# Choosing between VectorE and GpSimd: by estimate for every instruction, or fixed except near the barriers

## Chip, cores and metric

One core of one Trainium2 chip. The metric is device microseconds of that core for one execution of the whole kernel; lower is better. For a core that works alone there is no second die to compare with, so a run counts as fast when it is within 1.5% of the fastest of its kernel.

## The reference

Two layers; each adds a linear attention with softmax features and then a gated feed-forward network without an activation, both behind a layer normalisation. S = 2048 tokens, D = 576, H = 32 heads of Dh = 18, F = 4608, all in bf16. Both layers use the same weights.

```python
pq = q @ w_phi ; pk = k @ w_phi                           # per head, 18 x 18
phi_q = concat([softmax(pq), softmax(-pq)], axis=-1)      # the same for phi_k
kv  = phi_k^T @ v ; z = sum over tokens of phi_k          # needs all tokens
o   = (phi_q @ kv) / (phi_q @ z + 1e-6)
x   = x + o @ wo                                          # attention, of layernorm(x)
x   = x + ((x_ln @ w_gate) * (x_ln @ w_up)) @ w_down      # feed-forward, x_ln = layernorm(x)
# twice
```

Because `kv` sums over all tokens, every layer has a **K phase** (all tokens' features of K), a **barrier** (kv complete), and then **Q tiles** (128 tokens each, 16 of them), which feed **feed-forward blocks** (two tiles each, 8 per layer). Layer 2's K tiles are worked off as layer 1's blocks end; its barrier comes after layer 1's last block.

## The kernel before

The kernel is a program of tasks (Python generators) that a **list scheduler** places on the engines when the kernel is built. Each operation carries an estimated duration in ns; the scheduler takes the operation that could start earliest (tasks of priority 10 and 11 get a head start of 300 and 800 ns), a task's priority breaks ties and decides who gets a free buffer first, and the instruction streams are then fixed in that order.

A request `"alt"` names several engines; the one whose estimated finish is earliest gets the work (VectorE's estimate is weighted by 1.2):

```python
for eng, ops in r[1]:
    ...
    e_ = max(self.free_at[eng], tr.ready_time(deps), th.t_ready)
    f_ = e_ + sum(o.dur for o in ops) * self.alt_cost[eng]
    if pick is None or f_ < pick[0]:
        pick = (f_, e_, eng, ops)
```

Every K or Q tile passes through `softmax_front`. Each tile has two branches, softmax(p) and softmax(-p), of 128 x 576:

```python
def softmax_front(self, st_, pz, Wm, km):
    ...                                        # projection on TensorE, copy to psb on ScalarE, max and min on VectorE
    yield ("alt", [(eng, [Op(dur, ... tensor_tensor(d1, p3, mxb, ALU.subtract) ...)])      # L861, first difference
                   for eng, dur in (("pool", 1170), ("dve", 675))])
    for h in range(2):
        yield ("alt", [(eng, [Op(dur, ... tensor_tensor(d2h, ph, mnbh, ALU.subtract) ...)])  # L868, second, in halves
                       for eng, dur in (("pool", 620), ("dve", 375))])
    ...                                        # exp on ScalarE, sums on VectorE (L880), reciprocal on ScalarE
    for br in range(2):
        yield ("alt", [(eng, [Op(dur, ... tensor_tensor(ev, ev, rb, ALU.mult) ...)])         # L894, scaling
                       for eng, dur in (("pool", 1150), ("dve", 675))])
```

The layer normalisation `t_ln` ends with such a choice too (L804, estimates 800 on GpSimd and 280 on VectorE).

After its front, a Q tile transposes both branches on TensorE (L1020), ScalarE copies them (L1023), TensorE multiplies by kv (L1041), VectorE divides (L1066, one buffer `o`), TensorE transposes the result (L1077), ScalarE copies it to `oT` (L1082), and TensorE projects it (L837). The gate and up products of a block are L1130, the down projection L1197 and L1200.

Who starts Q tiles, and when:

```python
self.NPS, ... self.NO = 3, ..., 1              # 3 softmax buffers psb, 1 buffer o
self.pace = (8, 4)                             # layer 1, layer 2
def t_q(self, L):
    for b in range(NB):                        # NB = 8 pairs of tiles
        ...
        if b >= self.pace[L - 1]:              # pair b waits for the end of feed-forward block b - pace
            yield ("wait", ("x2", L, b - s.pace[L - 1]))
        if b >= s.early // 2:
            yield ("wait", ("BD", L))          # the barrier
        for j in range(2):
            yield ("go", s.t_aout(L, 2 * b + j), (4 if b == 0 else 7) + (NS - 2 * b - j) / 100.0, ...)
        ...                                    # cut: the pair's normalisation; from pair 1 on, a wait until the pair before is done
```

## Time and profile before

| | before |
|---|---|
| median of the first 3 runs | 1230.62 us (1229.88 to 1232.37) |
| end of layer 1's K phase (last L925 of it) | 104.9 us |
| first feed-forward matmul (first L1130) | 133.98 us |
| block starts, layer 1, blocks 2 to 7 | 61.3 to 62.0 us apart |
| block starts, layer 2, blocks 2 to 5 | 63.8 to 63.9 us apart |

The lines of the page, the stages and the groups stand in the prediction. Timeline columns: start, duration, engine, line, operation, how often; in brackets the idle time before it and what ended it. Every Q tile has one L1082 copy, when its output is ready for the last projection.

```profile
114.06 0.69 ACT L1082 COPY oT<-ps 128x640 bf16<-128x640 bf16 x1 [2.19 <-PE ps L1077]
126.46 0.69 ACT L1082 COPY oT<-ps 128x640 bf16<-128x640 bf16 x1 [0.90 <-PE ps L1077]
...
133.98 0.28 PE L1130 MATMUL ps<-xT,Wg 64*128 64x256 bf16 x1 [0.78 <-ACT xT L818]
```

Block 0 starts at 134.

The four scalings of one pair of layer 2's Q tiles, the timeline of the kernel before from 909 to 913 us, GpSimd and VectorE:

```profile
909.17 1.16 POOL L894 TENSOR_TENSOR dd<-dd,ss 128x576 bf16<-128x576 bf16 x1 [2.60 <-ACT ss L888]
909.85 2.74 DVE L894 TENSOR_TENSOR dd<-dd,ss 128x576 bf16<-128x576 bf16 x2
910.58 1.39 POOL L894 TENSOR_TENSOR dd<-dd,ss 128x576 bf16<-128x576 bf16 x1 [0.25 <-ACT ss L888]
```

VectorE's two take 2.74 us where two of 0.745 would take 1.5: both engines work by turns. TensorE's waits in layer 2's Q blocks, 732 to 1056 us, before (total, times, longest):

```profile
PE ps L1020 <- DVE dd L894: 4.5, 5, 1.1
PE ps L1197 <- DMA wdr<-in_B_w_down_dram: 4.3, 9, 1.0
PE ps L1020 <- POOL dd L894: 1.3, 2, 1.2
```

### The profile page before, as it was taken

To read this page: it belongs to the slowest core of one execution; us is meant where nothing else is said; L and a number is where in the kernel's file an instruction comes from. 1 tells how busy PE (TensorE), PEld (TensorE's weight loads), DVE (VectorE), ACT (ScalarE), POOL (GpSimd) and SP (SyncE) were. 2 spreads that over 40 slices of the span, in tenths; PEclk is the share of its full clock that TensorE was granted. 3 is DMA by queue.
4 is the path that set the end of the run, shared out by engine and by line. 5 is a ranking of instruction groups with operands and counts; after the bars stand their busy time and mean duration, and the time that the engine had idled before them with its cause. 6 is when DMAs were issued, how large, how long until landed. Compare 5 with 4: busy or idle time off the path is not lost.

```text
span 1227.8 us, 33685 instructions
## 1 busy us (share of the span) xinstructions
PE 1131.8 (92%) x15202; PEld 846.5 (69%) x15202; DVE 663.3 (54%) x1243; ACT 460.1 (37%) x1080; POOL 233.3 (19%) x225
## 2 busy tenths in 40 slices
PE   5775999998999999999999589999999999999998
PEld 3553786875858585858586368685867677767684
DVE  7898658679444444444446684836353635422131
ACT  6766446364323232323224444424242424212120
POOL 4686205234020202020203320302010101000000
PEclk8888899999999999999999789999999999999999
DMA  8372006216150515151514101604334342433414
GB/s 190 85 270 93 2 22 167 33 42 160 31 164 24 165 23 163 25 158 30 156 31 137 39 2 27 154 29 124 83 99 98 88 108 74 123 89 97 137 50 145
DMA packets 126249, 114.61 MB, mean 93 GB/s; under 512 B 44826, under 2 KB 124954, under 8 KB 124954
## 3 DMA queue, kind: packets, MB, share of 16 engines
q1 hardware_dynamic: 126106, 112.48, 33.7%
q8 instruction: 118, 1.93, 0.7%
q14 instruction: 25, 0.20, 0.1%
HBM read 100.59 MB, written 2.36 MB: 84 GB/s over the span
## 4 chain that ended last, share of the span: by engine, by line
PE 71%; DVE 14%; DMA 9%; ACT 3%; POOL 1%; issue 1%; SPq 0%; DVEq 0%; ACTq 0%
PE ps L1130 45%; PE ps L1197 10%; PE ps L837 9%; DMA wdr<-in_B_w_down_dram 9%; DVE dd L894 3%; DVE ss L880 2%; DVE dd L868 2%; DVE mxmn L856 2%; DVE mxmn L854 1%; PE ps L1200 1%; DVE st L782 1%; PE ps L1041 1%; PE ps L1020 1%; DVE xln L804 1%; PE ps L925 1%; PE ps L1077 1%
## 5 line engine op out<-in xcount | busy, mean ns | idle before, releaser
L1130 PE MATMUL ps<-xT,Wu 64*128 64x256 bf16 x4608 | 571.2, 270 | 2.0 <-DVE hT L1175 1.8
L1130 PE MATMUL ps<-xT,Wg 64*128 64x256 bf16 x4608 | 571.0, 270 | 1.6 <-ACT xT L818 1.6
L1130 PEld LDWEIGHTS ps<-xT,Wg 64*128 64x128 bf16 x4608 | 430.3, 94 | 33.8 <-issue 3.6
L1130 PEld LDWEIGHTS ps<-xT,Wu 64*128 64x128 bf16 x4608 | 432.5, 94 | 30.2 <-DVE hT L1175 3.1
L1175 DVE TENSOR_TENSOR hT<-ps,gsb 128x512 bf16<-128x512 f32 x288 | 198.6, 691 | 333.6 <-ACT gsb L1173 333.4
L1173 ACT CAST gsb<-ps 128x512 bf16<-128x512 f32 x288 | 168.5, 585 | 505.1 <-PE ps L1130 504.5
L1197 PE MATMUL ps<-wdr,hT 128*128 128x512 bf16 x1152 | 311.1, 381 | 15.9 <-DMA wdr<-in_B_w_down_dram 14.4
L1200 PE MATMUL ps<-wdr,hT 128*128 128x64 bf16 x1152 | 221.9, 193 | 0.0
L1197 PEld LDWEIGHTS ps<-wdr,hT 128*128 128x128 bf16 x1152 | 112.5, 98 | 152.8 <-DMA wdr<-in_B_w_down_dram 40.2
L861 POOL TENSOR_TENSOR dd<-psb,mxmn 128x576 bf16<-128x576 bf16 x63 | 75.8, 1203 | 566.5 <-DVE mxmn L854 566.4
L1130 PE MATMUL ps<-xT,Wr 64*128 64x256 bf16 x1152 | 168.5, 270 | 0.0
L1200 PEld LDWEIGHTS ps<-wdr,hT 128*128 128x128 bf16 x1152 | 112.9, 98 | 1.1
L894 POOL TENSOR_TENSOR dd<-dd,ss 128x576 bf16<-128x576 bf16 x69 | 96.2, 1398 | 90.9 <-ACT ss L888 90.8
L880 DVE TENSOR_REDUCE ss<-dd 128x64 f32<-128x1152 bf16 x64 | 85.9, 1343 | 8.6 <-ACT dd L875 8.1
L1221 DVE TENSOR_TENSOR x_sb<-ps,x_sb 128x512 bf16<-128x512 f32 x32 | 21.9, 684 | 119.5 <-PE ps L1200 119.5
L1130 PEld LDWEIGHTS ps<-xT,Wr 64*128 64x128 bf16 x1152 | 66.1, 94 | 7.0
L894 DVE TENSOR_TENSOR dd<-dd,ss 128x576 bf16<-128x576 bf16 x59 | 62.5, 1072 | 8.1 <-ACT ss L888 8.1
L1023 ACT COPY eT<-ps 126x512 bf16<-126x512 bf16 (+1 forms) x128 | 52.8, 423 | 22.0 <-PE ps L1020 19.3
L849 ACT CAST psb<-ps 128x288 bf16<-128x288 f32 x128 | 49.6, 396 | 27.7 <-PE ps L837 25.8
L873 ACT ACTIVATE dd<-dd 128x576 bf16<-128x576 bf16 x64 | 43.6, 681 | 41.6 <-DVE dd L868 30.2
L925 PE MATMUL ps<-vx,dd 128*126 128x127 bf16 (+1 forms) x320 | 30.4, 241 | 30.6 <-POOL dd L894 15.7
L854 DVE TENSOR_REDUCE mxmn<-psb 128x32 f32<-128x576 bf16 x64 | 47.2, 739 | 18.1 <-ACT psb L849 18.1
(82 smaller groups left out, 1017.2 us busy)
## 6 DMA issues: line engine op xcount, KB each, us to landing
wdr<-in_B_w_down_dram SPq DMA_DIRECT2D x288, 288.0 KB, 3.3
Wg<-in_B_w_gate_dram SPq DMA_DIRECT2D x4, 1152.0 KB, 12.7
Wu<-in_B_w_up_dram SPq DMA_DIRECT2D x4, 1152.0 KB, 15.5
x_sb<-in_A_x_dram SPq DMA_DIRECT2D x8, 288.0 KB, 3.3
out_dram<-x_sb SPq DMA_DIRECT2D x8, 288.0 KB, 3.7
Wraw<-in_A_wqkv_dram SPq DMA_DIRECT2D x8, 144.0 KB, 3.2
xT<-xln SPq DMA_TRANSPOSE x58, 2.7
Wv<-in_A_wqkv_dram SPq DMA_DIRECT2D x1, 576.0 KB, 4.3
```

Source lines behind the costliest of these rows:

```text
L837: ops.append(Op(d_pe(n), (lambda e, lhsT=lhsT, rhs=rhs, k=k: e.matmul(s.ps[:, bank, 0:n], lhsT, rhs, start=(k == 0), stop=(k == 4))), read ...
L849: yield ("ops", "act", [Op(d_actc(288), (lambda e, h=h, bank=bank: e.copy(psb[:, pz, 288 * h:288 * h + 288], s.ps[:, bank, 0:288])), reads ...
L854: yield ("ops", "dve", [Op(680, (lambda e: e.tensor_reduce(mxmn[:, pz, 0, :], p3, AX.X, ALU.max)), reads=[("psb", pz, 0), ("psb", pz, 1)], ...
L861: yield ("alt", [(eng, [Op(dur, (lambda e: e.tensor_tensor(d1, p3, mxb, ALU.subtract)), reads=[("psb", pz, 0), ("psb", pz, 1), ("mx", pz)] ...
L880: Op(1320, (lambda e: e.tensor_reduce(ss[:, sm, :].rearrange("p (b g) -> p b g", b=2), e4, AX.X, ALU.add)), reads=s.ddk(sm, 0) + s.ddk(sm, ...
L894: yield ("alt", [(eng, [Op(dur, (lambda e, ev=ev, rb=rb: e.tensor_tensor(ev, ev, rb, ALU.mult)), reads=s.ddk(sm, br) + [("ss", sm)], write ...
L1023: yield ("ops", "act", [Op(dur, (lambda e, et=et, P=P, r=r, t0=t0, t1=t1: e.copy(s.eT[0:r, et, t0:t1, :], P[0:r, 128 * t0:128 * t1].rearra ...
L1130: out.append(Op(54.3, (lambda e, bank=bank, cs=cs, lhsT=lhsT, rhs=rhs, st=st, sp=sp: e.matmul(ps[:, bank, cs], lhsT, rhs, start=st, stop=s ...
L1173: yield ("ops", "act", [Op(540, (lambda e, g=g, gb=gb: e.copy(gsb[:, g, :], ps[:, gb, :])), reads=[("gu", gb)], writes=[("gsb", g)], excl= ...
L1175: yield ("ops", "dve", [Op(625, (lambda e, g=g, ub=ub, p=p: e.tensor_tensor(hT[:, p, :], ps[:, ub, :], gsb[:, g, :], ALU.mult)), reads=[(" ...
L1197: ops.append(Op(d_pe(512), (lambda e, lhsT=lhsT, bank=bank, slot=slot, fi=fi, f=f: e.matmul(ps[:, bank, 0:512], lhsT, s.wdr[:, slot, fi, 0 ...
L1200: ops.append(Op(d_pe(64) + 3, (lambda e, lhsT=lhsT, sl=sl, slot=slot, fi=fi, f=f: e.matmul(ps[:, Z, 64 * sl:64 * sl + 64], lhsT, s.wdr[:, ...
```

## The change

Its intent: a choice by estimate mixes VectorE and GpSimd where they disturb each other and where estimates are wrong. Let the choice stand only where latency counts, next to the barriers (and, for the second difference, in layer 1's whole K phase); elsewhere scaling, first difference and normalisation go to GpSimd and the second difference to VectorE. `crit` is 2 for the last two K tiles of a layer, 1 for layer 1's other K tiles, 0 for the rest and for all Q tiles. Besides that, three estimates change and layer 1's Q pairs are paced.

```diff
-        self.pace = (8, 4)
+        self.pace = (5, 4)
 # t_ln: normalisation; spread=True at layer 1's start, pair 0, and the last two tiles of layer 2's K
-                for eng, dur in (("pool", 800), ("dve", 280))])
+                for eng, dur in (("pool", 800), ("dve", 340))[:1 + spread]])
 # softmax_front(..., crit)
-                       for eng, dur in (("pool", 1170), ("dve", 675))])
+                       for eng, dur in (("pool", 1150), ("dve", 675))[:1 + (crit > 1)]])
-                           for eng, dur in (("pool", 620), ("dve", 375))])
+                           for eng, dur in (("dve", 375), ("pool", 640))[:1 + (crit > 0)]])
-                           for eng, dur in (("pool", 1150), ("dve", 675))])
+                           for eng, dur in (("pool", 1150), ("dve", 675))[:1 + (crit > 1)]])
 # K tiles, Q tiles
-        sm = yield from s.softmax_front(st_, ps_, s.Wk, "Wk")
+        sm = yield from s.softmax_front(st_, ps_, s.Wk, "Wk", 2 if st_ >= NS - 2 else 1 if L == 1 else 0)
-        sm = yield from s.softmax_front(st_, ps_, s.Wq, "Wq")
+        sm = yield from s.softmax_front(st_, ps_, s.Wq, "Wq", 0)
 # (cut: the four calls of t_ln that pass spread=True)
```

More of the change, by code (lines that the diff above doesn't have):

```diff
@@ L767, in t_fuse2, with t_ln @@
         yield ("sig", ("w", which))
-    def t_ln(self, tiles, sig, fast=False):
+    def t_ln(self, tiles, sig, fast=False, spread=False):
         s = self
@@ L839, in proj, with softmax_front @@
         return ops
-    def softmax_front(self, st_, pz, Wm, km):
+    def softmax_front(self, st_, pz, Wm, km, crit):
         s = self
@@ L1244, in pair_done @@
             if b == 0:
-                yield ("go", s.t_ln([0], [("xTB1", L)], True), 11, "lnB%d_0a" % L)
+                yield ("go", s.t_ln([0], [("xTB1", L)], True, True), 11, "lnB%d_0a" % L)
                 yield ("wait", ("x1", L, 1))
-                yield ("go", s.t_ln([1], [("xTB2", L)], True), 11, "lnB%d_0b" % L)
+                yield ("go", s.t_ln([1], [("xTB2", L)], True, True), 11, "lnB%d_0b" % L)
                 yield ("wait", ("xTB1", L))
@@ L1277, in lns @@
                     yield ("wait", ("ain", 1, 2 * b - s.lnlead))
-                yield ("go", s.t_ln([2 * b, 2 * b + 1], [("xT", 1, b)]), 7, "lnA1_%d" % b)
+                yield ("go", s.t_ln([2 * b, 2 * b + 1], [("xT", 1, b)], False, True), 7, "lnA1_%d" % b)
         yield ("go", lns(), 7, "lns")
@@ L1300, in k2 @@
                     yield ("wait", ("x2t", L, 2 * b + j))
-                    yield ("go", s.t_ln([2 * b + j], [("xTk", j)], True), 11, "k2ln%d" % j)
+                    yield ("go", s.t_ln([2 * b + j], [("xTk", j)], True, True), 11, "k2ln%d" % j)
                 for j in range(2):
```

## The prediction

> **What bounds the kernel now.** I read the page first (busy shares, then the slices), then a table of busy time by stage, then the groups of the lines that the change touches, then single instructions in order of time, and last TensorE's waits by stage.
>
> ```profile
> span 1227.8 us, 33685 instructions
> PE 1131.8 (92%) x15202; PEld 846.5 (69%) x15202; DVE 663.3 (54%) x1243; ACT 460.1 (37%) x1080; POOL 233.3 (19%) x225
> PE   5775999998999999999999589999999999999998
> DVE  7898658679444444444446684836353635422131
> POOL 4686205234020202020203320302010101000000
> PEclk8888899999999999999999789999999999999999
> ```
>
> The slices show three kinds of time: the first four (the K phase of layer 1, to about 107 us, where DVE and POOL are high and PE is 5 to 7), a dip at slices 22 and 23 (the barrier before the second layer's Q phase), and the rest, where PE is 9. The table by stage puts numbers on it (columns: PE, weight load, DVE, ACT, POOL, granted clock, DMA):
>
> ```profile
> 0.00:107.00 107.00, 74.26 (x610) 51.12 (x610) 94.48 (x159) 71.78 (x207) 68.43 (x76) 0.88 0.61 183
> 107.00:134.00 27.00, 15.34 (x129) 11.16 (x129) 17.86 (x42) 14.55 (x41) 10.97 (x12) 0.76 0.00 1
> 134.00:310.00 176.00, 170.90 (x2309) 132.29 (x2311) 134.19 (x297) 91.59 (x224) 52.87 (x50) 1.00 0.30 75
> 665.00:732.00 67.00, 46.31 (x440) 31.02 (x439) 48.05 (x85) 29.43 (x77) 21.64 (x19) 0.85 0.17 49
> 732.00:1056.00 324.00, 313.30 (x4394) 239.16 (x4391) 169.15 (x342) 116.87 (x254) 36.69 (x34) 1.00 0.34 91
> ```
>
> TensorE is idle 32.7 us in the K phase, 11.7 at the first barrier, 5.1 to 310 us, 20.7 around the second barrier and 10.7 in the Q phase of layer 2; the rest of its 96 us (1227.8 less 1131.8) lies in stages that DMA waits end. So two thirds of the run can gain almost nothing from VectorE or GpSimd, and only the K phase (DVE busy 94.5 of 107 us) and the barriers are bound by those engines.
>
> **How the two engines meet.** The groups by line, with least, median and longest duration of one:
>
> ```profile
> L868 DVE TENSOR_TENSOR dd<-psb,mxmn x65: 394/555/1419, 31.5 to 1034.6; 128x288 bf16<-128x288 bf16 x65
> L868 POOL TENSOR_TENSOR dd<-psb,mxmn x63: 666/674/1192, 20.2 to 1032.4; 128x288 bf16<-128x288 bf16 x63
> L894 POOL TENSOR_TENSOR dd<-dd,ss x69: 1152/1228/1765, 28.6 to 1038.4; 128x576 bf16<-128x576 bf16 x69
> L894 DVE TENSOR_TENSOR dd<-dd,ss x59: 745/804/1720, 29.2 to 1038.7; 128x576 bf16<-128x576 bf16 x59
> ```
>
> The scatter is one of queueing, as four neighbours in the K phase show:
>
> ```profile
> 86.82 1.28 DVE L894 TENSOR_TENSOR dd<-dd,ss 128x576 bf16<-128x576 bf16 x1
> 88.03 1.41 DVE L868 TENSOR_TENSOR dd<-psb,mxmn 128x288 bf16<-128x288 bf16 x1
> 89.36 0.74 DVE L894 TENSOR_TENSOR dd<-dd,ss 128x576 bf16<-128x576 bf16 x1
> 86.33 2.80 POOL L894 TENSOR_TENSOR dd<-dd,ss 128x576 bf16<-128x576 bf16 x2
> ```
>
> GpSimd's two scalings alone would take 2 x 1.16 us and took 2.80; a VectorE half that takes 0.445 us alone took 1.41 and ended with the second of them; the scaling after it, with GpSimd idle, took 0.74. Whichever starts second waits for the other. In the whole run I sorted VectorE's instructions by overlap with a GpSimd one: L868 0.446 us alone and 0.843 beside one, L894 0.746 and 1.080, L804 (the normalisation) 0.425 and 0.788, while reductions (L880, 1.343) don't care. An operation moved from one engine to the other therefore does not buy parallel time, only a different owner.
>
> **What the skill says.** The Trainium skill's page "GPSIMD Engine Reference", section "1. Specifications", says GpSimd shares its SBUF interfaces with VectorE, with contention for VectorE instructions that have two SBUF inputs or a two-port mode. The trace agrees and gives the size above. The same page, section "4.1 Engine selection", calls GpSimd about twice as slow for elementwise work with two inputs; here it is 1.165 against 0.745 us (1.56 times) for 576 elements and 0.67 against 0.445 for 288. "TensorE: Matmul & The Clock Gate", "Part 1: The HAM clock gate", says an idle TensorE falls to half clock; the granted 0.76 and 0.85 at the two barriers agree, so a microsecond lost there costs some more afterwards.
>
> **The change part by part.** The kernel emits its instruction streams from a list scheduler that knows estimated durations; "choice" means that it takes the engine with the earlier estimated finish. Estimates themselves change little (340 for 280 ns on VectorE's normalisation).
>
> (1) Scaling, L894: 59 of 128 are on VectorE. Afterwards only the last two K tiles of each layer (8 instructions) may choose; I expect 124 on GpSimd. (2) Second difference, L868: 63 of 128 halves are on GpSimd; afterwards only layer 1's K tiles and the last two of layer 2 (36 halves) may choose, so about 13 stay. (3) Normalisation: 42 of 64 tiles become fixed on GpSimd (22 near the start and barriers may choose), about 47 against 15 now. (4) First difference, L861: 63 of 64 are there already. (5) Layer 1's Q pairs 5, 6, 7 wait for feed-forward blocks 0, 1, 2 to end; before, no pair waited.
> GpSimd: 233 + 55 x 1.165 - 50 x 0.67 + 32 x 0.82 = 290 us. VectorE: 663 - 55 x 1.06 + 50 x 0.75 - 32 x 0.53 = 625 us. Neither share matters as such; by stage:
>
> K phase. From the same groups by stage, 16 scalings and 12 halves are on VectorE there, 18 and 24 on GpSimd; of VectorE's 31.9 us in these two lines and the normalisation, 22.4 is its own (16 x 0.745 + 12 x 0.445 + 12 x 0.425) and 9.5 waiting. After: two or so scalings stay (-14 x 0.745 = -10.4), 14 halves come (+6.2): own work -4.2 us. But those 14 halves now meet GpSimd with a first difference or a scaling of 1.165 us in progress, and a half beside one waited 0.4 us on average: +14 x 0.4 = 5.6, and scalings on VectorE waited little, 0.16 us each, so -2. Sum -1. On GpSimd +14 x 1.165 - 14 x 0.67 = +7 of 107 us, and the matmuls that follow the scaling (L925) get its two branches in series, 2.33 us:
>
> ```profile
> PE ps L925 <- POOL dd L894: 15.7, 8, 5.8
> ```
>
> I take +2 for that; together +1 us.
>
> First barrier: Q tiles 0 and 1 lose their choice, the two K tiles keep it; TensorE's waits there are on ACT and VectorE copies, not on scaling (0.3 us). 0, give or take 3. From 134 to 425 us: 14 Q tiles run now between blocks 0 and 2, with DVE at 24 of 27 and 52 of 55 us; pacing moves four of them to the next two gaps, where it is at 12 of 26. At most the 5.1 us idle there can come back; I take -3. Layer 1's K tiles of the second layer have their products 11 us before the next block needs them, so 1.2 us more of GpSimd chain is hidden: 0. Second barrier: its tiles keep the choice: 0. Layer 2's Q blocks: two tiles scale on both engines at once, and TensorE waits about 1 us per block for the slow one (the four take 3.41 us, by the scheduler's estimates 2.5):
>
> ```profile
> PE ps L1020 <- DVE dd L894: 1.0, 1, 1.0
> ```
>
> On GpSimd the four take 4.66 us as estimated, so the matmuls are placed where the data is ready and down projections fill the gap. The Q result then comes 1.2 us later with some 5 us to spare before the next block. The six gaps before L1020 sum to 5.6 us; I take half, -3. Sum: +1 + 0 - 3 + 0 + 0 - 3 = -5 us, 1230.6 - 5 = 1225.6.
>
> **Rivals.** A: GpSimd becomes the bound of the K phase. It would be busy 75 of 107 us there and in series with each tile; for it speaks that 15.7 us of TensorE's waits there are already on its scaling, against it that VectorE is fuller (94.5). If its chain ends last per tile, 16 tiles x 0.7 us: 1236 to 1242. B: contention is the real loss, and an orderly split removes it. VectorE lost some 40 us in the whole run beside GpSimd; if the K phase regained its 9.5 and each barrier 4, with less cold clock, 1205 to 1212. Against: one engine still owns the port while the other waits, and halves on VectorE wait more than scalings do. C: nothing, since TensorE sets the end in most stages: 1228 to 1232. The streams are also reshuffled wholesale, worth several us either way at the barriers.
>
> **Range and chances.** Predicted 1225 us. The terms have errors of about 6 (K phase), 3 and 3 (barriers), 3 and 2; some 8 together, widened because a new order may do anything at a barrier: 1210 to 1240. Over 2% faster is under 1206, which needs B in full: 0.07. Over 2% slower is over 1255, which needs more than A: 0.04. Within: 0.89.
>
> **What would show it.** Right: 120 or more of L894 on GpSimd; VectorE's total near 625 and GpSimd's near 290 us; L868 on VectorE with a median above 0.6 us; the K phase ending between 103 and 113 us; the gaps before L1020 in layer 2's Q blocks at half; blocks 4 to 7 of layer 1 still starting 61.3 to 62.0 us apart (from the chain). Wrong: a K phase or a barrier that is over 8 us shorter or longer, or TensorE waiting for L894 on GpSimd inside a block.

## More of the kernel before

Pair 0 is started before the barrier with the low priority 4, so that it doesn't hold up the last K tiles; the later pairs have priority 7. Tiles 0 and 1 rise to 11 only when the barrier is passed and their own transposes (L1020) are emitted.

## The result, and the profile after

The changed kernel takes 1232.42 us (median of 4 runs, 1229.87 to 1233.79), the kernel before 1230.41 us on the same chip (4 runs). Ratio 1.0011, 95% interval 0.9991 to 1.0031: the same. Ratios here are the mean time of one kernel's fast runs over that of the other's of the same rounds, so not quite the ratio of the medians quoted.

From the page of the changed kernel:

```profile
span 1229.9 us, 33653 instructions
PE 1131.1 (92%) x15202; PEld 846.9 (69%) x15202; DVE 633.8 (52%) x1215; ACT 459.1 (37%) x1077; POOL 270.0 (22%) x256
PEclk9997799999999999999999979999999999999999
```

The groups of the two lines that moved most, after (least, median, longest of one):

```profile
L868 DVE TENSOR_TENSOR dd<-psb,mxmn x119: 399/452/1422, 21.4 to 1037.0; 128x288 bf16<-128x288 bf16 x119
L868 POOL TENSOR_TENSOR dd<-psb,mxmn x9: 671/737/1182, 21.4 to 702.8; 128x288 bf16<-128x288 bf16 x9
L894 POOL TENSOR_TENSOR dd<-dd,ss x123: 1156/1164/1736, 27.2 to 1042.7; 128x576 bf16<-128x576 bf16 x123
L894 DVE TENSOR_TENSOR dd<-dd,ss x5: 759/894/1716, 98.1 to 707.6; 128x576 bf16<-128x576 bf16 x5
```

So the engines did what the diff says. GpSimd has 36.7 us more busy time than before, VectorE 29.5 us less, and the time did not move. **Where it went**, I take from a balance by stage. For each kind of TensorE matmul I take the step at which it usually follows itself when nothing holds it up (the 30th percentile, from the kernel before), add these up between two milestones and subtract the sum from the time that passed. The rest is loss; it doesn't depend on which work the schedule put into the stage.

| from, to | loss before | loss after | difference |
|---|---|---|---|
| start, end of layer 1's K phase | 48.2 | 51.1 | +2.9 |
| K phase, first feed-forward matmul | 18.3 | 24.7 | +6.4 |
| blocks 0 to 4 of layer 1 | 15.3 | 16.4 | +1.2 |
| blocks 4 to 7 of layer 1 | 8.4 | 7.9 | -0.5 |
| block 7, end of layer 2's K work | 20.5 | 17.7 | -2.7 |
| layer 2, barrier and blocks 0 to 5 | 29.4 | 23.3 | -6.1 |
| layer 2, block 5 to the end | 12.4 | 13.5 | +1.0 |
| span | | | +2.1 |

It is a large gain in layer 2 and a large loss at the first barrier, and smaller terms. One profile of each kernel stands behind the table: ten kernels with the same instructions in the K phase ended it within 3.6 us of each other (more of this below), so terms of up to 3 us are not told from such scatter. The loss can be seen in the stages (columns as in the prediction), after:

```profile
107.00:134.00 27.00, 14.62 (x112) 10.31 (x111) 18.09 (x42) 14.11 (x37) 12.74 (x11) 0.62 0.00 1
665.00:732.00 67.00, 48.05 (x417) 30.71 (x417) 45.50 (x85) 29.43 (x77) 23.20 (x20) 0.87 0.28 80
732.00:1056.00 324.00, 317.87 (x4495) 243.92 (x4489) 158.74 (x334) 119.96 (x262) 57.58 (x54) 1.00 0.34 90
```

TensorE is busy 317.9 of 324 us in layer 2's Q blocks (313.3 before); at the first barrier the granted clock is 0.62 (0.76 before). The same lines of ScalarE's and TensorE's timeline as before:

```profile
115.92 0.69 ACT L1082 COPY oT<-ps 128x640 bf16<-128x640 bf16 x1 [2.91 <-PE ps L1077]
132.72 0.69 ACT L1082 COPY oT<-ps 128x640 bf16<-128x640 bf16 x1 [0.25 <-PE ps L1077]
139.30 0.69 ACT L1082 COPY oT<-ps 128x640 bf16<-128x640 bf16 x1 [0.80 <-PE ps L1077]
141.95 0.69 ACT L1082 COPY oT<-ps 128x640 bf16<-128x640 bf16 x1 [1.96 <-PE ps L1077]
...
148.36 0.28 PE L1130 MATMUL ps<-xT,Wg 64*128 64x256 bf16 x1 [0.78 <-ACT xT L818]
```

Four Q tiles come out before block 0 can start, not two. In the emitted order they are tiles 0, 2, 3 and 1: **tile 1, which block 0 needs, has been overtaken by the tiles of pair 1**. Building both kernels again and logging what the scheduler emits shows where: in both, tile 1 is given its softmax buffers before tiles 2 and 3 get theirs; but its second difference is emitted before the barrier in the kernel before, and behind those of tiles 2 and 3 in the changed one, where it has to be on VectorE. Block 0 starts 14.4 us later: 3.0 us by the later end of the K phase, 5.0 us of Q work done in advance, and the 6.4 us of loss. And layer 2: the scalings of the same pair of tiles, the timeline of GpSimd, and TensorE's waits in 732 to 1056 us, after:

```profile
913.30 4.53 POOL L894 TENSOR_TENSOR dd<-dd,ss 128x576 bf16<-128x576 bf16 x4 [3.76 <-ACT ss L888]
```

```profile
PE ps L1020 <- POOL dd L894: 2.4, 3, 0.8
PE ps L1197 <- DMA wdr<-in_B_w_down_dram: 1.9, 5, 0.6
PE ps L1041 <- ACT eT L1023: 0.7, 1, 0.7
```

The four scalings take 1.1 us longer than before (4.53 against 3.41 us from 909.17 to the end of VectorE's second at 912.58), and yet TensorE's waits on them are 3.4 us shorter in these five blocks and those on weights 2.4 us.

### The profile page after: what moved, and what is told of

It reads as the page before. It is cut to its first block, busy times and chain, and to the rows that moved or that the text cites. A ratio compares the mean times of both kernels' runs of the same rounds, so it can differ in the third digit from the quotient of the medians.

```text
span 1229.9 us, 33653 instructions
## 1 busy us (share of the span) xinstructions
PE 1131.1 (92%) x15202; PEld 846.9 (69%) x15202; DVE 633.8 (52%) x1215; ACT 459.1 (37%) x1077; POOL 270.0 (22%) x256
## 4 chain that ended last, share of the span: by engine, by line
PE 73%; DVE 13%; DMA 8%; ACT 4%; POOL 1%; issue 1%; SPq 0%; DVEq 0%; ACTq 0%
PE ps L1130 45%; PE ps L1197 12%; PE ps L837 9%; DMA wdr<-in_B_w_down_dram 8%; DVE dd L868 4%; DVE mxmn L854 2%; DVE mxmn L856 2%; DVE ss L880 2%; PE ps L1200 2%; PE ps L1020 1%; PE ps L1041 1%; POOL dd L894 1%; PE ps L925 1%; PE ps L1077 1%; DVE st L782 1%
## 5 line engine op out<-in xcount | busy, mean ns | idle before, releaser
L1197 PE MATMUL ps<-wdr,hT 128*128 128x512 bf16 x1152 | 311.3, 381 | 14.0 <-DMA wdr<-in_B_w_down_dram 12.7
L894 POOL TENSOR_TENSOR dd<-dd,ss 128x576 bf16<-128x576 bf16 x123 | 145.7, 1209 | 114.3 <-ACT ss L888 113.7
L1130 PE MATMUL ps<-xT,Wr 64*128 64x256 bf16 x1152 | 163.0, 270 | 0.0
L868 DVE TENSOR_TENSOR dd<-psb,mxmn 128x288 bf16<-128x288 bf16 x119 | 79.0, 698 | 0.7
L804 POOL TENSOR_SCALAR xln<-x_sb,nmean,rstd 128x576 bf16<-128x576 bf16 x47 | 39.1, 840 | 178.6 <-ACT rstd L800 178.6
L1130 PEld LDWEIGHTS ps<-xT,Wr 64*128 64x128 bf16 x1152 | 61.1, 94 | 7.0
L849 ACT CAST psb<-ps 128x288 bf16<-128x288 f32 x128 | 49.8, 398 | 31.4 <-PE ps L837 29.5
```

What stands on the lines that cost most here:

```text
L868: yield ("alt", [(eng, [Op(dur, (lambda e, d2h=d2h, ph=ph, mnbh=mnbh: e.tensor_tensor(d2h, ph, mnbh, ALU.subtract)), reads=[("psb", pz, h) ...
L894: yield ("alt", [(eng, [Op(dur, (lambda e, ev=ev, rb=rb: e.tensor_tensor(ev, ev, rb, ALU.mult)), reads=s.ddk(sm, br) + [("ss", sm)], write ...
L1130: out.append(Op(54.3, (lambda e, bank=bank, cs=cs, lhsT=lhsT, rhs=rhs, st=st, sp=sp: e.matmul(ps[:, bank, cs], lhsT, rhs, start=st, stop=s ...
L1197: ops.append(Op(d_pe(512), (lambda e, lhsT=lhsT, bank=bank, slot=slot, fi=fi, f=f: e.matmul(ps[:, bank, 0:512], lhsT, s.wdr[:, slot, fi, 0 ...
```

## The experiments

The theory after the first look: **(T1)** the first barrier costs by the overtaking of tile 1; **(T2)** layer 2 gains because the schedule now knows how long the scalings take, not because the engines stop disturbing each other or because GpSimd is better; **(T3)** pacing gives some 3 us. Rivals: the barrier loses because Q tiles 0 and 1 have lost VectorE's fast scaling; layer 2 gains by the absence of collisions; the K phase is bound by GpSimd.

All time ratios are to the kernel before in the same 5 rounds, with 95% intervals. The kernel before had medians of 1230.4 to 1233.0 us.

### What the first barrier costs

**after_q1first**: the changed kernel, with pair 1 held until tile 1's front is done.

```diff
             if b >= s.early // 2:
                 yield ("wait", ("BD", L))
+            if b == 1:
+                yield ("wait", ("qf", L, 1))
```

> The kernel after, with one wait of the emission order added: Q tiles 2 and 3 of a layer are only launched once the front of Q tile 1 is emitted. Theory 1 (order): the first barrier's extra 6.4 us (the first feed-forward matmul at 148.4 us after against 134.0 us before, 4.2 us more idle TensorE between the end of the K phase and that matmul, the rest colder clock) come from tiles 2 and 3 overtaking tile 1 for a softmax buffer, by priority. Then the first feed-forward matmul starts below 138 us, with at most 12 us of idle TensorE in that stage, and the total is about 1226 us, 6 below the kernel after and 4 below the kernel before. Rival (the fixed GpSimd scaling of the Q tiles is itself what is slow there): the start stays above 143 us or the idle time of that stage at 14 us or more, the total at 1230 to 1233.

Measured: 0.9990 (0.9970 to 1.0010), 1231.08 us. Only two tiles come out before block 0 now, and the first feed-forward matmul is at 140.0 us, not 148.4. By the balance the stage from the K phase to it loses 21.1 us: of the 6.4 us that the change lost there, 3.7 are back. TensorE's waits for L894 on GpSimd before L1020 in 104 to 152 us are 2.9 us (5.1 in the changed kernel, 0.3 before). So the overtaking is real and, by the balance, more than half of the loss, and not all of it. The expectation was missed in its numbers (below 138 us, 1226 us): the total is 1231.08 us, and its ratio of 0.9990 is not clear of the changed kernel's 1.0011. Block 0 starts 8.3 us earlier, but with less Q work done in advance; block 4 starts at 438.1 us, against 438.6 in the changed kernel. So what the order costs reaches the total clearly only in kernels further below (q1_fixed, est_only). The expectation's "for a softmax buffer" is not what that log shows either: tile 1 holds its buffers and loses its turn on the engines.

**q1_fixed** and **k1_fixed**: the kernel before, with the fixed engines in layer 1's Q tiles alone, or with first difference and scaling on GpSimd in layer 1's K tiles alone (but the last two).

```diff
+# fix=1: first difference and scaling on GpSimd; fix=2: also the second difference on VectorE
-        sm = yield from s.softmax_front(st_, ps_, s.Wq, "Wq")
+        sm = yield from s.softmax_front(st_, ps_, s.Wq, "Wq", 2 if L == 1 else 0)                  # q1_fixed
-        sm = yield from s.softmax_front(st_, ps_, s.Wk, "Wk")
+        sm = yield from s.softmax_front(st_, ps_, s.Wk, "Wk", 1 if L == 1 and st_ < NS - 2 else 0) # k1_fixed
```

> The kernel before, with only layer 1's Q tiles fixed (first difference and scaling on GpSimd, second on VectorE), no pacing. Theory: this part alone makes tile 1 fall behind tiles 2 and 3 at the first barrier: the first feed-forward matmul at 145 us or later (134.0 before), the loss up to it 5 to 7 us more than before, and 2 to 4 us more between the first and the fifth block (as the kernel after without pacing): total +7 to +10 us, ratio 1.006 to 1.008. Rival (the late K phase of the kernel after is what lets the tiles overtake): first feed-forward matmul at 138 us or earlier.

> The kernel before, with only layer 1's K tiles (but the last two) fixed as after: first difference and scaling on GpSimd, second difference free. Theory K (this is what lengthens the K phase by 3 us): the last product of that phase ends at 107 to 109 us against 104.9 before; the total +2 to +5 us, ratio 1.002 to 1.004. Rival (the 3 us come from the Q tiles 0 and 1, whose fronts lie at the end of that phase, or from the normalisation): it ends at 105.5 or less.

Measured: q1_fixed 1.0096 (1.0073 to 1.0118), 1244.19 us, the slowest of all: four tiles before block 0, which starts at 153.5 us. k1_fixed 1.0027 (1.0007 to 1.0047), 1236.01 us: its K phase ends at 104.2 us in its one profile, no later than before, so nothing shows GpSimd as the bound of the K phase when it has all first differences and scalings there; but again four tiles come out before block 0, which starts at 142.2 us. By the balance the stage loses 30.0 us in q1_fixed and 22.1 in k1_fixed, against 18.3 before.

**est_only**: the kernel before, every choice left in place, with only the estimates of the change.

```diff
-                for eng, dur in (("pool", 800), ("dve", 280))])
+                for eng, dur in (("pool", 800), ("dve", 340))])
-                       for eng, dur in (("pool", 1170), ("dve", 675))])
+                       for eng, dur in (("pool", 1150), ("dve", 675))])
-                           for eng, dur in (("pool", 620), ("dve", 375))])
+                           for eng, dur in (("dve", 375), ("pool", 640))])
```

> The kernel before with its free choice everywhere, and only the scheduler's estimates of the kernel after (1150 for 1170, 640 for 620 and 340 for 280 ns, ties to VectorE). Theory O (tile 1 falls behind tiles 2 and 3 at the first barrier because any small change of estimates or engines moves the moment at which it asks for a buffer; the rule of engines isn't needed for it): the first feed-forward matmul at 140 us or later, loss of that stage 21 to 25 us against 18.3, ratio 1.002 to 1.006. Rival (the rule that fixes the Q tiles' engines is what delays tile 1): first feed-forward matmul at 134 to 136 us, ratio 0.998 to 1.001.

Measured: 1.0073 (1.0051 to 1.0094), 1241.46 us. Four tiles come out before block 0, which starts at 150.5 us; in the emitted order they are 0, 2, 3 and 1 again. The stage loses 27.6 us by the balance, 9.3 more than before and more than expected, about what the total lost (0.73% are 9.0 us). The last of them in est_only, in ScalarE's timeline:

```profile
143.02 0.69 ACT L1082 COPY oT<-ps 128x640 bf16<-128x640 bf16 x1 [3.62 <-PE ps L1077]
```

No rule about engines is in this kernel. Three estimates that differ by 20 to 60 ns, and the order of one list, are enough to turn the order at this place, where pair 0 stands with priority 4 against 7 (that the priority lets it happen is read from the code; no run changes the priority alone). This is the clearest result on the barrier: the engine rule is not needed for the overtaking. Every kernel here that changed estimates or engines of layer 1's K or Q tiles before the barrier and did not pin the order turned it (five with the changed kernel and after_nopace); the twelve that left these alone kept it.

**after_q1first_choice**: the rival for the rest of the barrier's loss. The mended kernel, with the choice given back to Q tiles 0 and 1.

```diff
-        sm = yield from s.softmax_front(st_, ps_, s.Wq, "Wq", 0)
+        sm = yield from s.softmax_front(st_, ps_, s.Wq, "Wq", 2 if st_ < 2 else 0)
```

> The kernel after, with tile 1 ahead of tiles 2 and 3 and the free choice of engines given back to Q tiles 0 and 1. With the order alone mended, 3.7 of the 6.4 us of the first barrier came back (first feed-forward matmul at 140.0 us, 12.6 us idle). If the rest is the serial scaling of these two tiles on GpSimd: the first feed-forward matmul at 136 to 138 us, idle time of that stage 10.5 to 11.5 us, ratio to before 0.996 to 0.998. If it is the later K phase and its cold clock alone: as without the choice, 0.999.

Measured: 1.0005 (0.9987 to 1.0023), 1233.42 us. Block 0 starts at 138.6 us, and the stage's loss is 18.9, that of the kernel before (18.3). So giving tiles 0 and 1 their choice back takes 2.1 us off the stage's loss in these two profiles. By which step is not shown: TensorE's wait for GpSimd's scaling before L1020 stayed at 2.7 us (2.9 without the choice), and block 0 missed the expected 136 to 138 us. It brought no time in total (expected 0.996 to 0.998): the K phase ended at 110.2 us in this profile and later stages gave the rest away.

### Why layer 2 gains

**q2_fixed**, **q2_dve_scale**: the kernel before, with fixed engines in layer 2's Q tiles alone. In the first the scaling is on GpSimd, as in the change, in the second on VectorE.

```diff
-        sm = yield from s.softmax_front(st_, ps_, s.Wq, "Wq")
+        sm = yield from s.softmax_front(st_, ps_, s.Wq, "Wq", L == 2)
-                           for eng, dur in (("pool", 1150), ("dve", 675))])
+                           for eng, dur in (("pool", 1150), ("dve", 675))[:1 if fix else 2]])   # q2_fixed
+                           for eng, dur in (("pool", 1150), ("dve", 675))[1 if fix else 0:]])   # q2_dve_scale
 # in both, first difference: [:1 if fix else 2], second: [1 if fix else 0:]
```

> The kernel before, with fixed engines in the Q tiles of layer 2 alone (first difference and scaling on GpSimd, second difference on VectorE). Theory: the 6 us that the kernel after gains between the first and the sixth feed-forward block of layer 2 come from this part alone: 1224.5 us, ratio to before 0.995, block period 63.0 us against 63.9. Rival (they come from a shift of work by the rest of the change, or from work given back later): 1229 to 1231, period 63.9.

> As the run that fixed the engines in layer 2's Q tiles alone (ratio 0.9946 to before, block period 63.0 us), but the scaling there on VectorE only, so that no scaling of a tile meets another on the other engine. Theory C (what hurt in the kernel before is that two scalings on two engines wait for each other, later than the emission order allowed for): the same gain or a little more, ratio 0.992 to 0.995, period 62.5 to 63.1, the idle time before the transposes of a block (0.95 us before) at 0.5 or less. Rival G (the gain comes from taking work off VectorE): at least half the gain is lost, ratio 0.997 or more, period 63.5 or more.

Measured: q2_fixed 0.9946 (0.9926 to 0.9966), 1226.72 us; q2_dve_scale 0.9961 (0.9943 to 0.9979), 1226.27 us. The gain needs nothing but layer 2's Q tiles, and their scaling may be on either engine.

**q2_split**, **q2_split_true**: one branch on each engine, so that the scalings of a tile collide on purpose; the differences are fixed as in the two runs above. The two kernels differ only in what the scheduler is told: the old estimates (1150 and 675), or durations close to those seen beside each other (1280 and 1400).

```diff
-                           for eng, dur in (("pool", 1150), ("dve", 675))])
+                           for eng, dur in (((("pool", 1150),), (("dve", 675),))[br] if fix else (("pool", 1150), ("dve", 675)))])   # q2_split
+                           for eng, dur in (((("pool", 1280),), (("dve", 1400),))[br] if fix else (("pool", 1150), ("dve", 675)))])  # q2_split_true
```

> A control: layer 2's Q tiles with the differences fixed as in the run before it, but the two scalings of a tile split by hand, the first branch on GpSimd, the second on VectorE, with the scheduler's old estimates (1150 and 675 ns). Theory C: no gain against the kernel before, ratio 0.998 to 1.001, block period 63.7 to 64.0. If fixing the differences was what helped: 0.995.

> The same split, so the same collisions, but the scheduler is told what the split takes on the chip in the trace of before (1280 ns on GpSimd, 1400 ns on VectorE, the means of 1.16 and 1.39, and of 1.10 and 1.71 us). Theory C1 (the collision costs nothing by itself; what costs is that TensorE's order was laid out for data that came earlier): most of the gain is there, ratio 0.994 to 0.996, block period 62.8 to 63.2. Theory C2 (the collision itself is on the path): as the control, ratio 0.998 to 1.001, period 63.7 or more.

Measured: q2_split 1.0004 (0.9981 to 1.0026), 1231.20 us; q2_split_true 0.9963 (0.9943 to 0.9983), 1227.12 us. In the total the split by hand with the old estimates gains nothing, and the same split with true durations gains about as much as either fixed engine. The scalings still collide in it: one on VectorE takes 1.17 us in the mean (1.22 in q2_split, 0.75 in q2_dve_scale, where none collide). TensorE's waits in 732 to 1056 us, summed over all lines that the view lists (0.2 us and more), agree: 10.9 us before, 9.5 in q2_split, 6.6 in q2_split_true, 5.6 in q2_dve_scale, 6.8 in q2_fixed, 5.7 in the changed kernel. **The larger part of what costs is that TensorE's order was laid out for data some 1 us earlier than it came.** Not all of it: blocks 2 to 5 start 63.3 to 63.5 us apart in q2_split (63.7 to 64.0 were expected), between the 63.8 to 63.9 before and the 62.9 to 63.1 of q2_split_true. So in the blocks some of the gain came with fixing the differences, or with the order that followed from it, and the total of q2_split hides that. T2 holds for the larger part.

**l2_fixed**: the kernel before, with fixed engines in all of layer 2: its K tiles (but the last two) and its Q tiles.

```diff
-        sm = yield from s.softmax_front(st_, ps_, s.Wk, "Wk")
+        sm = yield from s.softmax_front(st_, ps_, s.Wk, "Wk", 2 if L == 2 and st_ < NS - 2 else 0)
-        sm = yield from s.softmax_front(st_, ps_, s.Wq, "Wq")
+        sm = yield from s.softmax_front(st_, ps_, s.Wq, "Wq", 2 if L == 2 else 0)
```

> The kernel before, with the fixed engines in all of layer 2 (K tiles but the last two, and Q tiles), layer 1 as before. If layer 2's K tiles add what the kernel after shows around the second barrier (2.7 us less loss), ratio 0.992 to 0.993, about 1222 us; if that belongs to the shifted work of the kernel after, as the run with Q tiles alone, 0.9946.

Measured: 0.9927 (0.9907 to 0.9946), **1221.78 us, the lowest time** (l2_late_ln below has a ratio that can't be told from it, 0.9930); the kernel before had 1230.43 us. Layer 1 up to its first barrier is emitted as before, two tiles come out before block 0, and it starts at 136.0 us.

**l2_d1dve**: l2_fixed with the first difference on VectorE too in the fixed tiles. In l2_fixed and in the changed kernel TensorE still waits 0.7 to 0.9 us for the scaling once in most blocks. There VectorE's half L868 starts while GpSimd is at the next tile's first difference (1.42 us for a half at 908.44 us in the changed kernel, 0.45 for its neighbour).

```diff
-                       for eng, dur in (("pool", 1170), ("dve", 675))[:1 if fix else 2]])
+                       for eng, dur in (("pool", 1170), ("dve", 675))[1 if fix else 0:]])
```

> An attempt at a better kernel: layer 2 fixed, with the first difference on VectorE too, so that of a tile only the scaling is on GpSimd and no VectorE half waits 0.97 us for a first difference on GpSimd. If that wait is what is left before the transposes (0.7 to 0.8 us per block): it falls below 0.3, block period 62.5 us, ratio 0.989 to 0.991. If the longer VectorE chain (0.745 us more per tile) takes its place: 0.992 to 0.994.

Measured: 0.9963 (0.9937 to 0.9989), 1226.42 us. The wait before L1020 is gone (0.2 us in the whole stretch), others have come in its place (DMA 4.9 us, L1041 1.2, L1077 1.1), and the sum is 8.8 us. The wait that was removed, in a stage with 61 us of TensorE work per 63 us, came back on other resources.

### What two engines at once can do

**contention**: not the reference's computation (a wrong result); a small kernel in which each kind of instruction runs 8 times per section, on VectorE alone, on GpSimd alone or on both at once (one profile, never timed against another kernel).

```python
V = [scale, None,  scale, reduce, tensor_scalar, tensor_scalar, half, half]   # VectorE, per section
P = [None,  scale, scale, scale,  None,          scale,         None, scale]  # GpSimd at the same time
```

> Not the computation: eight instructions of each kind on VectorE, on GpSimd, or on both at once (the result is wrong on purpose). Theory (one instruction with two SBUF inputs or a fast one-input form at a time, the second waits for the whole of the first): scalings of 576 elements take 0.745 us on VectorE alone and 1.165 on GpSimd alone; eight on each at once take the sum, 8 x 1.9 = 15.3 us of overlap; a scaling beside half-width subtractions or the normalisation the same way, 8 x 1.6 = 12.9 and 8 x 1.6 = 12.7 us; reductions beside GpSimd's scalings keep their 0.74 us. Rival (bandwidth is shared, so both slow down a little): eight on each at once take 10 to 12 us.

Measured: its timeline, 8 scalings on VectorE alone, 8 on GpSimd alone, then 8 on each at once (VectorE's line):

```profile
13.94 5.44 DVE L41 TENSOR_TENSOR dv<-x_sb,ss 128x576 bf16<-128x576 bf16 x8 [4.00 <-POOL dp L66]
19.55 9.00 POOL L41 TENSOR_TENSOR dp<-x_sb,ssp 128x576 bf16<-128x576 bf16 x8 [5.72 <-DVE dv L41]
28.68 13.16 DVE L41 TENSOR_TENSOR dv<-x_sb,ss 128x576 bf16<-128x576 bf16 x8 [9.30 <-POOL dp L41]
```

5.44 and 9.00 us alone; 13.2 us together, where full overlap would be 9.0 and strict turns 14.4. They alternate: each VectorE scaling takes 1.71 us instead of 0.75, each on GpSimd 1.67 instead of 1.16. Turns overlap a little, by 1.2 us in all or 0.08 per instruction, so the expected 15.3 us, a sum of recorded durations, was too long. Halves are alike: one takes 1.41 us instead of 0.45 beside GpSimd, and 8 and 8 take 10.8 us (3.0 and 9.0 alone, 12.9 expected). Reductions stay at 0.74, as expected. A tensor_scalar like the normalisation's is different: it takes 1.26 us instead of 0.42, but GpSimd's scaling beside it only 1.22 instead of 1.16. GpSimd's 8 scalings beside 8 of them:

```profile
54.07 9.61 POOL L41 TENSOR_TENSOR dp<-x_sb,ssp 128x576 bf16<-128x576 bf16 x8 [3.08 <-DVE dv L47]
```

The two together take 9.7 us, where strict turns would take 11.8 (2.80 and 9.00) and 12.7 were expected: here VectorE waits and GpSimd hardly does. The Trainium skill's page "SBUF — State Buffer", section "SBUF: two separate sides", calls the shared port pair "an **exclusive lock**, not a bandwidth split"; the times of scalings and halves agree, and beside a tensor_scalar GpSimd is held up for far less than that instruction's duration. For scalings and differences an alternative engine is therefore hardly a second lane; for a normalisation it is one in part.

### Pacing

**pace_only**, **after_nopace**, **l2_pace**: pacing alone in the kernel before, pacing undone in the changed kernel, pacing added to l2_fixed.

```diff
-        self.pace = (8, 4)       # pace_only, l2_pace: (5, 4);  after_nopace: back from (5, 4) to (8, 4)
+        self.pace = (5, 4)
```

> The kernel before with the pacing of layer 1's Q pairs alone (5 in place of 8). My prediction's step: up to 3 us less idle TensorE between the first and the fifth feed-forward block, 1227.5 us. Rival 1 (TensorE has the same work in every case and its idle time moves with the Q pairs): 1230 to 1231. Rival 2 (Q tiles that scale on both engines, put into blocks that were free of them, bring a wait of 0.9 us per block): 1231.5 to 1234.

> The kernel after with the pacing undone (8 in place of 5). If pacing gains 3 us in this company, 1235.5; if it gains nothing, 1232.4; if the deferred pairs cost about 0.8 us in each of the two later gaps and the pile-up of Q tiles does no harm, 1230.5. The first feed-forward matmul starts at 148 us in every case, since pacing touches nothing before it.

> The kernel with layer 2's engines fixed (ratio 0.9927), plus the pacing of the kernel after. As with pacing alone in the kernel before (ratio 1.0055): 4 to 6.5 us are lost between the first and the fifth feed-forward block, TensorE 4 us idle in each of the third and fourth gap: ratio 0.996 to 0.999. If pacing only hurt beside the free choice in layer 2's K tiles, which now are fixed: 0.993.

Measured: pace_only 1.0055 (1.0033 to 1.0077), 1239.31 us; l2_pace 1.0010 (0.9984 to 1.0037), 1231.79 us, that is 0.8% behind l2_fixed; after_nopace 1.0015 (0.9993 to 1.0037), 1236.43 us, no different from the changed kernel's 1.0011. So pacing costs 7 to 10 us in two kernels and nothing in the third. T3 falls. In pace_only the two stretches between the starts of blocks 2, 3 and 4 lose 6.2 and 5.6 us (2.7 and 2.3 before), and TensorE waits there for weights of the down projection. TensorE's largest wait in 290 to 435 us, before and in pace_only, one fence each:

```profile
PE ps L1197 <- DMA wdr<-in_B_w_down_dram: 1.3, 4, 0.4
```

```profile
PE ps L1197 <- DMA wdr<-in_B_w_down_dram: 5.0, 4, 2.1
```

**l2_late_fixed**: l2_pace, with layer 1's Q tiles from 10 on, those that pacing moves, fixed as in the change.

```diff
-        sm = yield from s.softmax_front(st_, ps_, s.Wq, "Wq", 2 if L == 2 else 0)
+        sm = yield from s.softmax_front(st_, ps_, s.Wq, "Wq", 2 if L == 2 or st_ >= 10 else 0)
```

> As the run with layer 2 fixed and pacing, but the Q tiles of the three deferred pairs of layer 1 (from tile 10 on) are fixed too. Theory C1 (a tile that scales on both engines inside a feed-forward gap makes TensorE wait, since the data comes later than the emission order assumed; fixed engines make it come as assumed): the two later gaps lose 3.6 to 4.0 us each in place of 5.6 to 6.2, ratio 0.992 to 0.994. Rival (the deferred tiles cost what they cost): as with pacing, 0.996 to 0.999.

Measured: 0.9987 (0.9965 to 1.0008), 1229.68 us. Fixed engines in the moved tiles do not remove the cost: 4.6 us of waits on weights in the same stretch (1.2 in the changed kernel), the two stretches still lose 5.5 us each. One thing that differed from the changed kernel was the sync queue: the two transposes of a normalisation, 2.52 us of issuing together, went out 6.7 us before the start of block 3 (at 355.85 us; block 3 at 362.59), in the changed kernel 4.3 us before it (363.97; 368.23), one more weight load ahead of them. And the normalisations there ran on VectorE in 6 of 8 tiles, in the changed kernel all on GpSimd.

**l2_late_ln**: l2_late_fixed with the change's rule for the normalisation.

```diff
-                for eng, dur in (("pool", 800), ("dve", 280))])
+                for eng, dur in (("pool", 800), ("dve", 280))[:1 + spread]])     # spread as in the change
```

> The kernel l2_late_fixed (layer 2 fixed, Q tiles from 10 on of layer 1 fixed, pacing 5) plus the change's rule for the normalisation: GpSimd unless the tile is one of those near the start and the barriers. Theory N: the 3 us that separate l2_late_fixed from the changed kernel in 290 to 435 us come from the normalisation of the tiles there being on VectorE, ready earlier, so that the sync queue issues their two transposes one weight chunk earlier. Then TensorE's waits on the down-projection weights in that stretch fall from 4.6 us to about 1.6, its two gaps between block starts shrink by 3 us together, and the ratio to before falls from 0.9987 to 0.996. Rival: where the transposes fall in the queue depends on the whole order of the schedule and not on that engine: the waits stay at 4 or more, the ratio between 0.998 and 1.002.

Measured: 0.9930 (0.9916 to 0.9944), 1224.26 us, with 1232.95 for the kernel before. The transposes go out 4.0 us before block 3 (355.68; 359.71), and the starts of blocks 2, 3 and 4 are 70.4 us apart instead of 72.2. TensorE's waits on weights in 290 to 435 us, l2_late_fixed, then l2_late_ln:

```profile
PE ps L1197 <- DMA wdr<-in_B_w_down_dram: 4.6, 5, 1.8
```

```profile
PE ps L1197 <- DMA wdr<-in_B_w_down_dram: 1.1, 4, 0.3
PE ps L1200 <- DMA wdr<-in_B_w_down_dram: 0.5, 2, 0.2
```

The waits fell to the 1.6 us expected, and with the rule pacing no longer costs much. It moved 3.6 us in the two stretches; the whole gained more than expected, 5 to 7 us, so something else in the order gained too; what, I have not traced.

**l2_ln**: the same rule on l2_fixed, that is with pacing as before.

```diff
-                for eng, dur in (("pool", 800), ("dve", 280))])
+                for eng, dur in (("pool", 800), ("dve", 280))[:1 + spread]])     # spread as in the change
```

> The fastest kernel so far (l2_fixed: layer 2's tiles fixed, pacing as before) plus the same rule for the normalisation. If the rule is harmless or helps the transposes' place in the queue: 0.990 to 0.994, a best version. If a different order at the first barrier lets tile 1 be overtaken again: 0.997 to 1.003, with the first feed-forward matmul after 140 us instead of 134.

Measured: 0.9962 (0.9945 to 0.9979), 1227.81 us: slower than l2_fixed, and neither of the two expectations. Two tiles come out first and block 0 starts at 135.2 us, but from block 2 to 3 it takes 66.8 us (61.1 in l2_fixed), with 4.7 us of waits on weights in 290 to 435 us, one of 3.0. The rule is thus no good in itself: with one pacing it shortens the waits on weights, with the other it lengthens them. What moved in the queue in l2_ln I have not traced.

## Why the prediction was right or wrong

The total was predicted 5 us faster and came out 1.4 us slower by the mean ratio; it lies inside the range and within 2%, but the direction was wrong. One term was missed (the first barrier), one had the wrong sign (pacing), and one was too small (layer 2); that the total stayed near zero is these cancelling.

**First barrier, "0, give or take 3": the step that failed.** Measured +6.4 us of loss. The prediction asked what the waits there are on, and found ScalarE and VectorE copies, not scaling. It took for granted that the tiles would keep their order. Tile 1 came out fourth instead of second (after_q1first: 3.7 us), and Q tiles 0 and 1 were slower without a choice (2.1 us more back in after_q1first_choice). est_only shows that the order can turn by estimates alone. The text said "a new order may do anything at a barrier", but put that into the width of the range, where a reading of the priorities, 4 for pair 0 against 7 for pair 1, would have shown what was at risk. Of its signs of being wrong, "a barrier that is over 8 us shorter or longer" did appear: from the end of the K phase to block 0 it took 40.4 us instead of 29.1. TensorE's waits for L894 on GpSimd before L1020 rose there too, from 0.3 to 5.1 us (in 104 to 152 us).

**From 134 to 425 us, "-3" by pacing: wrong sign.** Alone it costs 7 to 10 us (pace_only, l2_pace). The step "at most the 5.1 us idle there can come back" counted what the early Q tiles leave behind in the first two stretches and not what they bring into the next two: there the moved tiles' normalisations put two transposes into the queue that loads the weights. In the changed kernel the stage ended at +1.2 us for blocks 0 to 4, with 1.2 us of waits on weights in 290 to 435 us; l2_late_ln suggests that the normalisation rule took the cost away there.

**Layer 2's Q blocks, "-3": right mechanism, size off.** Measured -6. The prediction named the estimate that was too short as the cause, and q2_split against q2_split_true shows that for the larger part. It took half of 5.6 us of waits on the scaling; these shrank by 3.4 us, from 5.8 to 2.4, so "the gaps before L1020 at half" held for their sum. It did not hold for the single gap: in three of the five blocks one of 0.72 to 0.84 us is left against 0.95 before, beside a collision of L868 with the next tile's first difference. Another 2.4 us came from waits on weights, which the prediction left out. Why these shrank is not shown: in q2_split_true and q2_dve_scale, which also gain, they stay at 4.4 and 4.0 us (4.3 before).

**K phase, "+1": not settled.** It ended 3.0 us later in the profile. The prediction gave +2 us to the waits on GpSimd's scaling, 15.7 us. They rose to 21.5, but it had left out 5.4 us of waits on VectorE's scaling, which are gone after: 21.1 and 21.5 us in all, with another owner. TensorE's waits in the K phase, before and after:

```profile
PE ps L925 <- POOL dd L894: 15.7, 8, 5.8
PE ps L925 <- DVE dd L894: 5.4, 6, 3.6
```

```profile
PE ps L925 <- POOL dd L894: 21.5, 12, 5.9
```

Nor did GpSimd fill up: it is busy 66.7 of the first 107 us (68.4 before; 75 predicted). Ten kernels with the same instructions in this phase (the kernel before among them) ended it between 104.6 and 108.2 us, one profile each; 107.9 lies inside. k1_fixed, with GpSimd at least as full as in the change (69.4 us), ended it at 104.2. Rival A, GpSimd as the bound, has nothing for it; whether the change costs 0 or 3 us here, single profiles cannot say.

**Second barrier and layer 2's K tiles, "0".** The balance shows -2.7 us from block 7 to the end of the K work. The same stage varies from 17.7 to 22.5 us over all kernels here; I have run nothing that isolates it.

**Counts.** Right: 123 scalings on GpSimd (predicted 124), 47 normalisations on GpSimd in its group (47), VectorE's total 633.8 (625), blocks 4 to 7 of layer 1 61.1 to 62.0 us apart. Wrong: GpSimd's total 270 (predicted 290), mostly because its scalings waited less: a mean of 1.21 us over the whole run instead of 1.40. The median of L868 on VectorE fell from 0.555 to 0.452 us (predicted over 0.6); its mean was 0.70, for 43 of 119 halves took over 0.6 us and those waited long. The prediction's sorting of VectorE's instructions by overlap, done again, gives somewhat less beside GpSimd for L868 (0.81 us) and L804 (0.74), and 55 of 59 L894 overlap one; nothing rests on the difference.

Rival B, the gain by an orderly split, is refuted as stated: 1205 to 1212 us did not come, and q2_split_true keeps the collisions and gains. Rival C, nothing, gives nearly the number (1228 to 1232) but not the reason: its parts are stages of -6 to +6 us, and their cancelling is luck. Alone, against the kernel before, layer 2 gives -0.7%, pacing +0.55%, layer 1's Q tiles +1.0%, its K tiles +0.3%, the estimates +0.7%. The rule for the normalisation was not run alone; it gave +0.35% on l2_fixed and -0.6% on l2_late_fixed. The five add up to +1.8% and the whole is +0.1%: effects through this list schedule didn't add.

## What to carry to other kernels

Where a scheduler lays out instruction streams from estimates, a wrong estimate costs on the engine that waits, not on the one that is estimated: first give it the duration that the trace shows under contention, and only then think of fixing engines (and compare the order of tiles after either: est_only moved three estimates and lost 0.7%). Keep a change of engines to the stage whose waits it addresses (here layer 2 alone, 0.7% faster, while the whole change gave nothing), because every other stage is reshuffled by it. And before changing anything upstream of a barrier, read which task's priority keeps the order there, and pin that order with an explicit wait (after_q1first shows that this restores the order; what it is worth in time on the fastest kernels has not been run); then look at what else shares the queue that brings the weights.

## What the Trainium skill lacked or had wrong

- "GPSIMD Engine Reference", section "4.1 Engine selection", gives about 2 times for elementwise work with two inputs. For the bf16 scaling with a broadcast f32 factor, alone, it is 9.00 against 5.44 us for 8, that is 1.65 times.
- The exclusive lock of "SBUF — State Buffer", section "SBUF: two separate sides", agrees with the runs for scalings (13.2 us for 8 and 8, 9.0 if they ran side by side). The page has the lock held for the whole instruction; measured by durations in the profile the other engine loses less: 8 tensor_scalar of 0.42 us each lengthened GpSimd's 8 scalings from 9.00 to 9.61 us. What it does not say, and is needed to read a profile: the time blocked is shown as duration of the instruction that waits (0.75 became 1.71 us on VectorE, 1.16 became 1.67 on GpSimd), not as idle time before it.
- "Perfetto Trace Analysis", section "GPSIMD Engine Instruction", calls a GpSimd instruction's span in a profile unreliable. For these two-input operations it was good: 1.16 us of duration against a step of 1.125 (9.00 us for 8).
- I found no page that has, for this chip and a DMA transpose of this size, how long it holds the issuing queue: two transposes of a normalisation (128 x 640 each) hold it for 2.52 us here. With one weight load more or less ahead of them TensorE's waits on weights were 1.6 or 4.6 us.
